# Second expert layer on Trainium2: the 64-token block contracted in two halves, side by side in the array

## The chip, the cores and the metric

One core of one Trainium2 chip runs the kernel. The metric is device microseconds of one launch: 1049.75 us, the median of three runs (1048.55 to 1050.27). Everything is float32 apart from small bfloat16 tiles of the assignment.

## The reference

The reference is an attention without softmax, followed by a mixture of experts in which each expert takes the same number of tokens. Only the last lines bear on the change: for each of E = 8 experts, the cap = 576 tokens that it was given go through two layers.

```python
out = np.einsum('bhsd,bhde->bhse', q, kv)          # kv = einsum('bhsd,bhse->bhde', k, v)
...
cap = N // E                                       # N 4608, E 8: cap 576
...
for e in range(E):
    mask = assigned == e
    h = np.maximum(x[mask] @ w1[e], 0.0)           # 576 x 512 by 512 x 1024
    out[mask] = h @ w2[e]                          # 576 x 1024 by 1024 x 512
```

## The kernel before

The kernel works in three stages. The **attention** (first 175 us) makes the tokens' rows and gate logits, batch by batch. Its last four token tiles are made of the last 64 tokens of two batches each: `token_tile` (L158) multiplies the two halves of such a tile, 64 tokens each, by the matrices `bd` of their two batches, and one half's result goes to partitions 0 to 63 of the PSUM tile `o_ps`, the other's to 64 to 127. The two halves alternate in the innermost loop. For the 32 other tiles one matmul has all 128 tokens. The **assignment** (to about 480 us) finds each token's expert, mostly on VectorE.

The **experts** follow, one after the other, and this is the stage that the change touches. An expert's 576 tokens are gathered in blocks of 128, 128, 128, 128 and 64 (list `blocks`), and turned by TensorE transposes (`turn`, L493) into `xt`. The first layer (L509) makes `hid`, 8 chunks of 128 units by 576 tokens, in matmuls of 288 columns. Then the next expert's tokens are turned and the tokens of the one after it gathered (`gather`, L482). The second layer (loop at L516) goes block by block: 8 matmuls, one for each chunk `f` of 128 of the 1024 units, add up in a PSUM tile `y_ps` of 512 columns (L519). The stationary operand is `hid` of the block's tokens, 128 or 64 columns wide, and the moving one is a chunk of `w2`. `take` moves the result to `y_sb`, and an indirect DMA writes it to the tokens' rows of the output (L523).

Two things set the order around the change. TensorE's instructions stand in the order in which the tile scheduler left them: an expert's second layer follows its first, with the next expert's transposes between the first blocks. And `take` gives every copy out of PSUM to ScalarE and VectorE in turn, by a counter that runs over the whole stage, so the number of copies in an expert decides which engine starts the next one. An expert has 16 copies of `hid`, 5 of `xt` and 5 of `y_sb`. The weights of expert e + 2 are loaded by SyncE as soon as the buffers of expert e are free (`load_w`, L189 and L191; two buffers each).

Each float32 matmul shows in the trace as two records on TensorE, each with a weight load of its own; the text calls such a record a pass.

Of the kernel before, what the change touches and what calls it, by code (L numbers as in the profile page):

```python
# [7 lines left out]
FT = mybir.dt.float32  # L8
# [3 lines left out]
AL = mybir.AluOpType  # L12
# [1 line left out]
AXX = mybir.AxisListType.X  # L14

P = 128
# Candidate thresholds that one counting step tries, and steps to a threshold: 17 ** -8 of the
# logits' range is below their last bit.
NCAND = 16
NSTEP = 8  # L20
NONE = -1.0e30
# [3 lines left out]
def kernel(  # L25
# [11 lines left out]
    nc = tc.nc  # L37
# [3 lines left out]
    N, DM = out.shape  # L41
    E, _, F = moe_w1.shape
    CAP = N // E
    NP = H // 2          # head pairs: two heads fill the 128 partitions
    J = 4                # consecutive tokens of a partition, in a batch's first 512
    G = J * P            # those tokens; the other S - G of two batches share a tile
    TL = S - G
    KP = 96              # k and v: S = 96 partitions of 6 rows
    KR = S // KP
    GC = N // P          # token tiles  # L50
    DC = DM // P
    FC = F // P
    W = 2 * (D + E)      # columns of a head pair: both kv, and both parts of the gate
    NB = (CAP + P - 1) // P
    HALF = CAP // 2
    assert TL * 2 == P and GC == B * J + B // 2 and HALF <= 512

    const = ctx.enter_context(tc.tile_pool(name="const", bufs=1, side="left"))
    wpool = ctx.enter_context(tc.tile_pool(name="wpool", bufs=2, side="left"))
# [5 lines left out]
    psa_cm = tc.tile_pool(name="ps_att", bufs=1, space=PS)  # L65
    psa = psa_cm.__enter__()

# [1 line left out]
    loaded = {}  # L69

    def load_kv(b):
# [25 lines left out]
    load_kv(1)  # L97
    load_q(1)

# [1 line left out]
    iota_p_i = const.tile([P, 1], I32, name="iota_p_i")  # L101
    nc.gpsimd.iota(iota_p_i, pattern=[[0, 1]], base=0, channel_multiplier=1)
    iota_p = const.tile([P, 1], FT, name="iota_p")
# [7 lines left out]
    nc.vector.tensor_scalar(gw.rearrange("p r l e -> p (r l e)"), in0=gw.rearrange("p r l e -> p (r l e)"),  # L111
                            scalar1=g_col, scalar2=None, op0=AL.mult)

    # Per batch and head pair, [kv, kv diag(g) w_gate], each with both heads on its diagonal.
    bd = att.tile([P, B, NP, W], FT, name="bd", bufs=1)
    nc.gpsimd.memset(bd[:, 0], 0.0)
    nc.gpsimd.memset(bd[:, 1:B], 0.0)
# [1 line left out]
    q_tail = att.tile([P, B // 2, H, D], FT, name="q_tail", bufs=1)  # L119
    lg = const.tile([P, E, GC], FT, name="lg")  # L120

# [1 line left out]
    def kv_product(b):  # L123
        k_sb, v_sb = loaded.pop(("k", b)), loaded.pop(("v", b))
        kv_ps = psa.tile([P, NP, D], FT, name="kv_ps", tag="kv")
# [15 lines left out]
        nc.vector.tensor_copy(bd[:, b, :, P:W], w_ps.rearrange("p r l e -> p r (l e)"))  # L141

    def token_tile(c, rows, batches, x_row):
        """rows(r): the tile's q of head pair r; batches: its one, or its two halves'."""
        qt_ps = psa.tile([P, NP, P], FT, name="qt_ps", tag="qt", bufs=2)
        for r in range(NP):
            nc.tensor.transpose(qt_ps[:, r, :], rows(r), ident)  # L147
        qt = att.tile([P, NP, P], FT, name="qt", tag="qt", bufs=3)
        if c % 2 == 0:
            nc.scalar.copy(qt, qt_ps)  # L150
        else:
            nc.vector.tensor_copy(qt, qt_ps)
        o_ps = psa.tile([P, NP, 256], FT, name="o_ps", tag="o", bufs=2)
        step = P // len(batches)
        for r in range(NP):
            for n, b in enumerate(batches):
                ps_ = slice(n * step, (n + 1) * step)
                nc.tensor.matmul(o_ps[ps_, r, 0:W], lhsT=qt[:, r, ps_], rhs=bd[:, b, r],  # L158
                                 start=True, stop=True)
        o_v = o_ps[:, :, 0:P]  # L160
        sq = att.tile([P, NP, P], FT, name="sq", tag="sq")
        nc.scalar.activation(sq, o_v, ACT.Square)  # L162
        ms = att.tile([P, H], FT, name="ms", tag="ms", bufs=3)
        nc.vector.reduce_sum(out=ms, in_=sq.rearrange("p r (l d) -> p (r l) d", l=2), axis=AXX)  # L164
        nc.vector.tensor_scalar(ms, in0=ms, scalar1=1.0 / D, scalar2=1.0e-6, op0=AL.mult, op1=AL.add)
        rt = att.tile([P, H], FT, name="rt", tag="rt", bufs=3)
        nc.scalar.activation(rt, ms, ACT.Sqrt)
        inv = att.tile([P, H], FT, name="inv", tag="inv", bufs=3)
        nc.vector.reciprocal(inv, rt)
        # One Newton step, as the table of the root is not exact.  # L170
        nc.vector.tensor_tensor(rt, inv, inv, op=AL.mult)
        nc.vector.tensor_tensor(rt, rt, ms, op=AL.mult)
        nc.vector.tensor_scalar(rt, in0=rt, scalar1=-0.5, scalar2=1.5, op0=AL.mult, op1=AL.add)  # L173
        nc.vector.tensor_tensor(inv, inv, rt, op=AL.mult)
        inv_h = inv.rearrange("p (r l o) -> p r l o", l=2, o=1)
        nc.vector.tensor_tensor(x_row.rearrange("p (r l d) -> p r l d", r=NP, l=2),
                                o_v.rearrange("p r (l d) -> p r l d", l=2),
                                inv_h.to_broadcast([P, NP, 2, D]), op=AL.mult)
        part = att.tile([P, NP, 2, E], FT, name="part", tag="part")
        nc.vector.tensor_tensor(part, o_ps[:, :, P:W].rearrange("p r (l e) -> p r l e", l=2),  # L180
                                inv_h.to_broadcast([P, NP, 2, E]), op=AL.mult)
        nc.vector.reduce_sum(out=lg[:, :, c], in_=part.rearrange("p r l e -> p e (r l)"), axis=AXX)

# [1 line left out]
    weights = {}  # L185

    def load_w(e):
# [34 lines left out]
    psa_cm.__exit__(None, None, None)  # L222
    att_cm.__exit__(None, None, None)

# [1 line left out]
    # Taking the logits from the highest down, until some expert is full: up to there every token  # L226
    # goes to its best expert that still has room. So E - 1 thresholds, in turn, and the rest.
    asg_cm = tc.tile_pool(name="asg", bufs=1, side="right")
    asg = asg_cm.__enter__()
    psr_cm = tc.tile_pool(name="ps_asg", bufs=1, space=PS)  # L230
# [17 lines left out]
    nc.vector.memset(inner, 1.0)  # L248
    nc.vector.memset(inner[:, :, 0:1], 0.0)

    # The logits' range, the same in every partition.
    ends = asg.tile([P, 2], FT, name="ends")
    lgf = lg.rearrange("p e c -> p (e c)")
    nc.vector.tensor_reduce(ends[:, 0:1], lgf, axis=AXX, op=AL.max)
# [35 lines left out]
        return asg.tile([P, w], dt, name=nm, tag="s_" + nm, bufs=2)  # L290

    def choose():
        """best: each token's best expert with room, of equals the first; mx: that logit, or
        below NONE / 2 for tokens that have their expert."""
        nc.vector.tensor_tensor(wl, lg, bc_e(shut), op=AL.add)
        nc.vector.tensor_reduce(mx, wl.rearrange("p e c -> p c e"), axis=AXX, op=AL.max)
        nc.vector.tensor_tensor(pick, wl, bc_c(mx), op=AL.is_ge)
        nc.vector.tensor_tensor(pick, pick, bc_e(code), op=AL.mult)
        nc.vector.tensor_reduce(code_mx, pick.rearrange("p e c -> p c e"), axis=AXX, op=AL.max)
        nc.vector.tensor_tensor(best, pick, bc_c(code_mx), op=AL.is_equal)  # L300
        nc.vector.tensor_tensor(mx, mx, gone, op=AL.add)

    def threshold():
        """[lo, hi) with an expert full when all at or above lo are taken, and none at hi."""
        lo, hi = bottom, top
        for _ in range(NSTEP):
            step = small("step")
# [26 lines left out]
        return lo, hi  # L334

    def ranks(own, sums):
        """For each token in `own`: one more than those before it of its partition, and how many
        there are in the partitions before."""
        here = asg.tile([P, E, GC], FT, name="here", tag="here", bufs=2)
        nc.vector.tensor_tensor_scan(here.rearrange("p e c -> p (e c)"), inner.rearrange("p e c -> p (e c)"),  # L340
                                     own.rearrange("p e c -> p (e c)"), 0.0, op0=AL.mult, op1=AL.add)
        ahead_ps = psr.tile([P, E], FT, name="ahead_ps", tag="end", bufs=2)
        nc.tensor.matmul(ahead_ps, lhsT=before, rhs=sums, start=True, stop=True)
        return here, ahead_ps

    def assign(lo, hi):
        """All at or above hi, and of those in [lo, hi) as many as their expert has room for."""
        two = asg.tile([P, 2, E, GC], BF, name="two", tag="two")
        cut = small("cut", GC)
        nc.vector.tensor_scalar(cut, in0=mx, scalar1=hi, scalar2=None, op0=AL.is_ge)  # L350
# [36 lines left out]
    nc.vector.tensor_tensor(pick, best, bc_c(rest), op=AL.mult)  # L387
    nc.vector.tensor_tensor(given, given, pick, op=AL.add)

# [1 line left out]
    sums_f = small("sums_f", 2 * E)[:, 0:E]  # L391
    nc.vector.reduce_sum(out=sums_f, in_=given, axis=AXX)
    sums = small("sums", 2 * E, BF)[:, 0:E]
# [17 lines left out]
    block = small("block", GC)  # L411
    nc.vector.tensor_copy(block, block_i)

    # The tokens' rows, in two numbers that bfloat16 holds.
    row_id = asg.tile([P, GC], I32, name="row_id")
    nc.gpsimd.iota(row_id[:, 0:B * J], pattern=[[S, B], [1, J]], base=0, channel_multiplier=J)
    nc.gpsimd.iota(row_id[:, B * J:GC], pattern=[[2 * S, B // 2]], base=G, channel_multiplier=1)
# [32 lines left out]
    psr_cm.__exit__(None, None, None)  # L450
    asg_cm.__exit__(None, None, None)

# [1 line left out]
    moe = ctx.enter_context(tc.tile_pool(name="moe", bufs=2, side="right"))  # L454
    psm = ctx.enter_context(tc.tile_pool(name="ps_moe", bufs=2, space=PS))

# [1 line left out]
    taken = {"n": 0}  # L458

    def take(dst, src, relu=False, scale=None):  # L460
        """Out of PSUM, on ScalarE and VectorE in turn."""
        taken["n"] += 1
        if taken["n"] % 2:
            if relu:
# [35 lines left out]
    for e in range(E):  # L500
# [14 lines left out]
            gather(e + 2)  # L515
        for n, (a, nr) in enumerate(blocks):  # L516
            y_ps = psm.tile([P, DM], FT, name="y_ps", tag="y")
            for f in range(FC):
                nc.tensor.matmul(y_ps[0:nr, :], lhsT=hid[:, f, a:a + nr], rhs=w2[:, f, :],  # L519
                                 start=(f == 0), stop=(f == FC - 1))  # L520
            y_sb = moe.tile([P, DM], FT, name="y_sb", tag="y", bufs=4)
            take(y_sb[0:nr, :], y_ps[0:nr, :])
            put = nc.gpsimd.indirect_dma_start(  # L523
                out=out, out_offset=bass.IndirectOffsetOnAxis(ap=ids[0:nr, e * NB + n:e * NB + n + 1], axis=0),
                in_=y_sb[0:nr, :], in_offset=None)
            tc.declare_no_dep(put.ins, group="rows_out", reason="every output row is written once")
            tc.add_to_no_dep_group("rows_out", put.ins)
# [30 lines left out]
```

## Time and profile before

| | |
|---|---|
| median of 3 runs | 1049.75 us (1048.55 to 1050.27) |
| span of the profiled execution, first to last instruction | 1045.8 us |
| its own time beside the span | the page gives none; the runs lie 2.8 to 4.5 us above the span |
| TensorE busy | 756.9 us (72%) |
| of it second layer, blocks of 128 tokens | 224.1 us in 512 passes |
| of it second layer, blocks of 64 tokens | 56.6 us in 128 passes |
| VectorE, ScalarE, GpSimd busy | 363.2, 98.7, 105.1 us |

The profile is one execution on the chip, and its span is the time between the first and the last instruction. Busy time of TensorE counts overlapping passes once. A group of rows names the source line, the engine, the operation, and output and input tiles.

### The profile page before, as it was taken

Reading aid. Unit: us, or ns where it says so; the run is one execution under the profiler, and the core shown is the slowest. Engines: PE = TensorE matmul, PEld = TensorE weight load, DVE = VectorE, ACT = ScalarE, POOL = GpSimd, SP = SyncE. Lnnn points to the kernel's source line nnn. Section 1 sums busy time; section 2 is a strip of 40 time slices with the busy share of each in tenths; the row PEclk is TensorE's granted clock in tenths of the full one; section 3 lists DMA queues with packets and bytes.
Section 4 is the critical chain, followed back from the end, with each engine's and each line's share of the span. In section 5 each row is a group of like instructions: output and inputs, shape, how many; then the busy total and the mean of one; then the engine's idle time right before and its main releaser. Section 6 shows DMA issues by size and latency. Waiting matters only on the chain.

```text
span 1045.8 us, 12692 instructions
## 1 busy us (share of the span) xinstructions
PE 756.9 (72%) x5277; PEld 509.7 (49%) x5277; DVE 363.2 (35%) x1295; ACT 98.7 (9%) x212; POOL 105.1 (10%) x132
## 2 busy tenths in 40 slices
PE   3796884223223223216999999999999999999996
PEld 3786874122212222213755747557466475574752
DVE  0666576565675666674110101101011011010100
ACT  1332231000000000000110101101001011010100
POOL 2211110000000000004120110210202100101001
PEclk9998796555555555555999999999999999999999
DMA  9999991000000000003133212330323122301000
GB/s 225 261 259 295 268 385 60 22 1 1 1 1 2 1 1 1 2 1 89 47 146 106 105 62 86 138 112 25 133 96 136 44 72 101 105 1 41 6 20 25
DMA packets 45721, 91.01 MB, mean 87 GB/s; under 512 B 7008, under 2 KB 27488, under 8 KB 44640
## 3 DMA queue, kind: packets, MB, share of 16 engines
q1 hardware_dynamic: 37632, 61.87, 20.8%
q0 software_dynamic: 7328, 28.32, 7.5%
q8 instruction: 41, 0.67, 0.3%
q10 hardware_dynamic: 704, 0.02, 0.1%
q14 instruction: 16, 0.13, 0.0%
HBM read 71.32 MB, written 18.87 MB: 86 GB/s over the span
## 4 chain that ended last, share of the span: by engine, by line
issue 50%; DVE 22%; PE 18%; POOL 6%; DMA 2%; ACT 2%; POOLq 0%; SPq 0%; DVEq 0%; ACTq 0%
PE n_ps L318 6%; PE o_ps L158 4%; DVE over L313 4%; POOL out_dram L523 4%; PE kv_ps L129 3%; POOL xg L482 2%; DVE cand L311 2%; DMA v_sb<-in_v_dram 1%; DVE up L328 1%; DVE step L308 1%; DVE hi L330 1%; PE qt_ps L147 1%; DVE lo L332 1%; PE k_ps L326 1%; DVE full L321 1%
## 5 line engine op out<-in xcount | busy, mean ns | idle before, releaser
L519 PE MATMUL y_ps<-w_sb,hid 128*128 128x512 f32 (+1 forms) x640 | 280.2, 594 | 0.0
L509 PE MATMUL h_ps<-xt,w_sb 128*128 128x288 f32 x1024 | 251.7, 408 | 0.0
L509 PEld LDWEIGHTS h_ps<-xt,w_sb 128*128 128x128 f32 x1024 | 194.5, 191 | 58.8 <-issue 5.7
L519 PEld LDWEIGHTS y_ps<-w_sb,hid 128*128 128x128 f32 (+1 forms) x640 | 112.5, 179 | 151.3 <-issue 150.7
L318 PE MATMUL n_ps<-best,over 128*16 128x8 bf16 x2016 | 62.5, 176 | 146.1 <-DVE over L313 105.5
L318 PEld LDWEIGHTS <-over 128*16 128x16 bf16 x2016 | 57.0, 89 | 173.9 <-DVE over L313 172.2
L471 DVE TENSOR_SCALAR hid<-h_ps 128x288 f32<-128x288 f32 x64 | 29.3, 458 | 253.2 <-PE h_ps L509 253.2
L475 DVE COPY y_sb<-y_ps 128x512 f32<-128x512 f32 (+1 forms) x17 | 11.8, 691 | 208.7 <-PE y_ps L519 208.7
L482 POOL DMA_INDIRECT xg<-x_dram,ids x40 | 37.9, 946 | 450.1 <-DVE ids L448 295.7
L158 PE MATMUL o_ps<-bd,qt 128*128 128x144 f32 (+1 forms) x320 | 54.9, 361 | 25.3 <-DVE rt L173 19.7
L523 POOL DMA_INDIRECT out_dram<-y_sb,ids x40 | 38.5, 964 | 323.6 <-ACT y_sb L469 189.4
L158 PEld LDWEIGHTS o_ps<-bd,qt 128*128 128x128 f32 (+1 forms) x320 | 49.2, 232 | 28.1 <-issue 24.7
L129 PE MATMUL kv_ps<-v_sb,k_sb 96*64 96x64 f32 x768 | 44.2, 242 | 14.4 <-DMA v_sb<-in_v_dram 14.4
L129 PEld LDWEIGHTS kv_ps<-v_sb,k_sb 96*64 96x64 f32 x768 | 41.4, 152 | 17.9 <-issue 16.2
L465 ACT ACTIVATE hid<-h_ps 128x288 f32<-128x288 f32 x64 | 26.3, 411 | 221.9 <-PE h_ps L509 221.9
L313 DVE TENSOR_TENSOR over<-mx,cand 128x576 bf16<-128x576 f32 x56 | 42.3, 755 | 1.5
L467 ACT ACTIVATE xt<-t_ps,g_col 128x512 f32<-128x512 f32 (+1 forms) x17 | 11.5, 675 | 326.3 <-DMA xg<-x_dram,ids 311.5
L469 ACT COPY y_sb<-y_ps 128x512 f32<-128x512 f32 (+1 forms) x23 | 13.4, 584 | 253.6 <-PE y_ps L519 253.6
L321 DVE SCALAR_TENSOR_TENSOR full<-n_ps,goal 16x8 f32<-16x8 f32 x56 | 8.6, 153 | 67.3 <-PE n_ps L318 67.3
L164 DVE TENSOR_REDUCE ms<-sq 128x8 f32<-128x512 f32 x36 | 24.6, 685 | 19.8 <-ACT sq L162 19.3
L162 ACT ACTIVATE sq<-o_ps 128x512 f32<-128x512 f32 x36 | 21.5, 597 | 73.1 <-PE o_ps L158 73.1
L473 DVE TENSOR_SCALAR xt<-t_ps,g_col 128x512 f32<-128x512 f32 (+1 forms) x23 | 15.4, 669 | 35.8 <-PE t_ps L493 33.8
(143 smaller groups left out, 471.6 us busy)
## 6 DMA issues: line engine op xcount, KB each, us to landing
w_sb<-in_moe_w_dram SPq DMA_DIRECT2D x16, 2048.0 KB, 9.7
k_sb<-in_k_dram SPq DMA_DIRECT2D x8, 1152.0 KB, 13.2
v_sb<-in_v_dram SPq DMA_DIRECT2D x8, 1152.0 KB, 18.1
q_sb<-in_q_dram SPq DMA_DIRECT2D x8, 1024.0 KB, 18.7
x_dram<-x_sb POOLq DMA_DIRECT2D x8, 1024.0 KB, 8.9
q_tail<-in_q_dram SPq DMA_DIRECT2D x8, 128.0 KB, 6.3
x_dram<-x_sb POOLq DMA_DIRECT2D x2, 512.0 KB, 5.4
xg<-x_dram,ids POOLq DMA_INDIRECT x40, 6.2
```

What stands on the lines that cost most here:

```text
L129: nc.tensor.matmul(kv_ps[ls, h // 2, :], lhsT=k_sb[:, h, j, :], rhs=v_sb[:, h, j, :], start=(j == 0), stop=(j == KR - 1))
L158: nc.tensor.matmul(o_ps[ps_, r, 0:W], lhsT=qt[:, r, ps_], rhs=bd[:, b, r], start=True, stop=True)
L162: nc.scalar.activation(sq, o_v, ACT.Square)
L164: nc.vector.reduce_sum(out=ms, in_=sq.rearrange("p r (l d) -> p (r l) d", l=2), axis=AXX)
L313: nc.vector.tensor_tensor(over, mx.rearrange("p (c o) -> p c o", o=1).to_broadcast([P, GC, NCAND]), cand.rearrange("p (o n) -> p o n", o=1 ...
L318: nc.tensor.matmul(n_ps, lhsT=over[:, c, :], rhs=best[:, :, c], start=(c == 0), stop=(c == GC - 1))
L465: nc.scalar.activation(dst, src, ACT.Relu)
L471: nc.vector.tensor_scalar(dst, in0=src, scalar1=0.0, scalar2=None, op0=AL.max)
L482: nc.gpsimd.indirect_dma_start(out=xg[0:nr, :], out_offset=None, in_=x_dram, in_offset=bass.IndirectOffsetOnAxis(ap=ids[0:nr, e * NB + n:e ...
L509: nc.tensor.matmul(h_ps, lhsT=w1[:, d, f * P:(f + 1) * P], rhs=xt[:, d, cs], start=(d == 0), stop=(d == DC - 1))
L519: nc.tensor.matmul(y_ps[0:nr, :], lhsT=hid[:, f, a:a + nr], rhs=w2[:, f, :], start=(f == 0), stop=(f == FC - 1))
L523: put = nc.gpsimd.indirect_dma_start(out=out, out_offset=bass.IndirectOffsetOnAxis(ap=ids[0:nr, e * NB + n:e * NB + n + 1], axis=0), in_=y ...
```

## The change

The 64-token block gets a branch of its own. Its 8 matmuls become 8 matmuls of the same shape, but the chunks of units 0 to 3 add up in partitions 0 to 63 of `y_ps`, and chunks 4 to 7 in partitions 64 to 127; the two alternate. Afterwards ScalarE copies the upper half to a new tile `y_part`, and VectorE adds it to the lower half into `y_sb`. The four 128-token blocks stay as they were. An expert thus has 25 copies that `take` counts, where it had 26. (The rest of the diff takes comments out and puts an assertion in.)

```diff
             y_ps = psm.tile([P, DM], FT, name="y_ps", tag="y")
-            for f in range(FC):
-                nc.tensor.matmul(y_ps[0:nr, :], lhsT=hid[:, f, a:a + nr], rhs=w2[:, f, :],
-                                 start=(f == 0), stop=(f == FC - 1))
             y_sb = moe.tile([P, DM], FT, name="y_sb", tag="y", bufs=4)
-            take(y_sb[0:nr, :], y_ps[0:nr, :])
+            if nr == P:
+                for f in range(FC):
+                    nc.tensor.matmul(y_ps, lhsT=hid[:, f, a:a + nr], rhs=w2[:, f, :],
+                                     start=(f == 0), stop=(f == FC - 1))
+                take(y_sb, y_ps)
+            else:
+
+                for f in range(FC // 2):
+                    for l in range(2):
+                        nc.tensor.matmul(y_ps[l * nr:(l + 1) * nr], lhsT=hid[:, l * FC // 2 + f, a:a + nr],
+                                         rhs=w2[:, l * FC // 2 + f, :], start=(f == 0), stop=(f == FC // 2 - 1))
+                y_part = moe.tile([P // 2, DM], FT, name="y_part", tag="y_part")
+                nc.scalar.copy(y_part, y_ps[nr:2 * nr])
+                nc.vector.tensor_tensor(y_sb[0:nr], y_ps[0:nr], y_part, op=AL.add)
```

On ScalarE, at the end of the first expert and through the second, the difference of the two programs' orders reads as follows (`h_ps`, `t_ps` and `y_ps` are the PSUM tiles of the first layer, the transposes and the second layer).

```order
 L467 ACTIVATE xt<-t_ps,g_col 128x4x128 x2
 L469 COPY y_sb<-y_ps 128x512 x2
-L469 COPY y_sb<-y_ps 64x512
+L531 COPY y_part<-y_ps 64x512
+L465 ACTIVATE hid<-h_ps 128x288 x8
+L467 ACTIVATE xt<-t_ps,g_col 128x4x128 x2
+L467 ACTIVATE xt<-t_ps,g_col 128x4x64
+L469 COPY y_sb<-y_ps 128x512 x2
+L531 COPY y_part<-y_ps 64x512
```

ScalarE keeps one instruction for the 64-token block, and every second expert it now has the copy of the short `xt` that VectorE had before.

On VectorE, at the end of the last expert, the addition stands in the place of a copy, and it comes after ScalarE's copy.

```order
 L471 TENSOR_SCALAR hid<-h_ps 128x288 x8
 L475 COPY y_sb<-y_ps 128x512 x2
-L475 COPY y_sb<-y_ps 64x512
-L553 UNCONDITIONAL_BRANCH
+L532 TENSOR_TENSOR y_sb<-y_ps,y_part 64x512
+L563 UNCONDITIONAL_BRANCH
```

The number of instructions before it is the same; the last one has a second input.

## Rows read from the trace of the kernel before

**Rows 1.** The page: engine totals, then the span in 40 slices.
```profile
PE 756.9 (72%) x5277; PEld 509.7 (49%) x5277; DVE 363.2 (35%) x1295; ACT 98.7 (9%) x212; POOL 105.1 (10%) x132
...
PE   3796884223223223216999999999999999999996
...
PEclk9998796555555555555999999999999999999999
```

**Rows 2.** Windows, nearly the whole experts' stage: length, busy time of each engine, clock.
```profile
526.00:1035.00 509.00, 509.00 (x1667) 295.85 (x1666) 49.88 (x93) 45.78 (x93) 60.81 (x64) 1.00 0.22 80
```

**Rows 3.** Groups by line and form, experts' stage: busy us, mean ns, idle before.
```profile
L519 PE MATMUL y_ps<-w_sb,hid 128*128 128x512 f32 x512 | 224.1, 594 | 0.0
...
L519 PE MATMUL y_ps<-w_sb,hid 128*64 128x512 f32 x128 | 56.6, 595 | 0.0
...
L519 PEld LDWEIGHTS y_ps<-w_sb,hid 128*64 128x64 f32 x128 | 16.9, 137 | 38.8 <-issue 38.8
```

**Rows 4.** Timeline of one 64-token block, expert 0: start us, us, instruction.
```profile
554.54 7.08 PE L519 MATMUL y_ps<-w_sb,hid 128*64 128x512 f32 x16
...
561.55 4.63 PE L509 MATMUL h_ps<-xt,w_sb 128*128 128x288 f32 x18
```

**Rows 5.** Timeline of the last block: weight loads, first and last of 14 single ones.
```profile
1029.05 0.14 PEld L519 LDWEIGHTS y_ps<-w_sb,hid 128*64 128x64 f32 x1 [0.29 <-issue]
...
1034.63 0.14 PEld L519 LDWEIGHTS y_ps<-w_sb,hid 128*64 128x64 f32 x1 [0.29 <-issue]
```

**Rows 6.** Windows of L158, a tile of one batch: PE busy (passes seen), PEld, clock.
```profile
28.40:28.60 0.20, 0.20 (x2) 0.20 (x2) 0.50 1.11 353
26.50:28.72 2.22, 1.98 (x9) 1.98 (x10) 0.61 1.08 316
26.50:28.96 2.46, 2.22 (x10) 2.22 (x11) 0.60 1.08 319
26.50:29.20 2.70, 2.46 (x11) 2.46 (x12) 0.59 1.08 323
...
141.40:141.72 0.32, 0.26 (x2) 0.29 (x3) 1.00 0.73 301
141.40:141.84 0.44, 0.38 (x3) 0.41 (x4) 1.00 0.80 317
141.40:141.96 0.56, 0.50 (x4) 0.54 (x5) 1.00 0.83 329
```

**Rows 7.** Windows of L158, tiles of two half batches; the same columns.
```profile
163.90:164.10 0.20, 0.14 (x2) 0.17 (x4) 0.50 0.00 0
163.90:164.34 0.44, 0.38 (x4) 0.41 (x6) 0.50 0.00 0
163.90:164.58 0.68, 0.62 (x6) 0.66 (x8) 0.50 0.00 0
...
170.90:173.90 3.00, 2.94 (x26) 2.97 (x28) 0.52 0.00 0
170.90:174.02 3.12, 3.06 (x28) 3.09 (x30) 0.54 0.00 0
170.90:174.14 3.24, 3.18 (x30) 3.21 (x32) 0.56 0.00 0
...
173.90:174.10 0.20, 0.20 (x8) 0.20 (x6) 1.00 0.00 0
```

**Rows 8.** Timeline, the end of the program.
```profile
1035.69 0.68 DVE L475 COPY y_sb<-y_ps 64x512 f32<-64x512 f32 x1 [13.19 <-PE y_ps L519]
1036.65 0.90 POOL L523 DMA_INDIRECT out_dram<-y_sb,ids  x1 [6.10 <-DVE y_sb L475]
```

**Rows 9.** Groups by line and form: prices of the copy and the addition.
```profile
L469 ACT COPY y_sb<-y_ps 64x512 f32<-64x512 f32 x7 | 4.1, 579 | 93.6 <-PE y_ps L519 93.6
...
L176 DVE TENSOR_TENSOR x_sb<-o_ps,inv 128x512 f32<-128x512 f32 x36 | 24.8, 688 | 1.4
```

**Rows 10.** Timeline of the attention's end: VectorE waits for ScalarE.
```profile
160.67 0.60 ACT L162 ACTIVATE sq<-o_ps 128x512 f32<-128x512 f32 x1 [1.00 <-PE o_ps L158]
...
161.30 0.69 DVE L164 TENSOR_REDUCE ms<-sq 128x8 f32<-128x512 f32 x1 [0.63 <-ACT sq L162]
```

**Rows 11.** DMA issues by line: KB each, median us to landing.
```profile
w_sb<-in_moe_w_dram SPq DMA_DIRECT2D x16, 2048.0 KB, 9.7
...
xg<-x_dram,ids POOLq DMA_INDIRECT x40, 6.2
out_dram<-y_sb,ids POOLq DMA_INDIRECT x40, 2.7
```

More of the change, by code (lines that the diff above doesn't have):

```diff
@@ L55 @@
     HALF = CAP // 2
-    assert TL * 2 == P and GC == B * J + B // 2 and HALF <= 512
+    assert CAP % P in (0, P // 2) and TL * 2 == P and GC == B * J + B // 2 and HALF <= 512
     const = ctx.enter_context(tc.tile_pool(name="const", bufs=1, side="left"))
```

## The prediction

> **What bounds the kernel now.** I first read the page's totals and its 40 slices. The totals call TensorE busy 72% of the span, an average over three stages. The slices split it: in the second half every slice of PE is a 9, at a granted clock of 9 or more, while the middle, the assignment, has PE at 2 or 3 [rows 1]. The change lies in the second half, so I asked for that stretch alone. In the 509 us from 526 to 1035 us TensorE is busy for 509.00 us, at clock 1.00, that is at 2.4 GHz; the four other engines have 46 to 61 us each, and the weight loads 296 us [rows 2]. Nothing else ends a wait there: TensorE is the bound, and a microsecond taken out of its queue is a microsecond off the end, until something else is late.
>
> Next the groups by form, since the mean over all forms would hide the point. Second-layer passes with 128 stationary columns and with 64 take the same 594 and 595 ns as records [rows 3]. A block of 64 tokens thus costs what one of 128 costs. The records overlap, so their lengths are not the pace. The pace is read from the weight loads, one to a pass: the first and last of 14 single ones begin at 1029.05 and 1034.63 us, so 5.58 / 13 = **0.429 us** a pass [rows 5]. Whole block: its first pass begins at 554.54, the next expert's first matmul at 561.55 us [rows 4], so 7.01 us, which is 16 x 0.429 = 6.86 and 0.15 for going into the narrow form and out of it.
>
> **The change, part by part.** *The matmuls.* Their number (16 passes a block, 8 blocks), shape and moving columns stay. Nothing is removed; the only possible gain is that two passes on different column halves run at once. The trace of before shows whether they do, in another place: the last four token tiles of the attention send 64 tokens to the lower half and 64 to the upper half of the same PSUM tile, alternating, in the same float32. I read it by windows that begin before the first pass and end at different times, so that the count tells how many passes have begun.
>
> First the control, a tile with all 128 columns. At clock 0.50 (1.2 GHz) the count goes 9, 10, 11 with every 0.24 us; at clock 1.00 it goes 2, 3, 4 with every 0.12 us [rows 6]. One pass at a time: 144 moving columns, 0.24 or 0.12 us. Then the half tiles: at clock 0.50 the count is 2, 4, 6 at 164.10, 164.34, 164.58, two with every 0.24 us, and two have begun already within the first window; the second pair of tiles, where the clock has risen to 1.00, goes 26, 28, 30 with every 0.12 us [rows 7]. Two passes begin where one did, at both levels of the clock, and the first two begin together. So the halves run fully beside each other here, with no offset that the view shows.
>
> I take this factor of two for the new block: 8 pairs x 0.429 = 3.43 us instead of 6.86, and the 0.15 us for the form stays. Saved: 3.43 us a block, 8 x 3.43 = **27.4 us**. What differs from the witness is the length, 512 columns for 144, and that four passes of a half add up in place; consecutive passes add up in place now at the full pace [rows 5]. Bounds of this term: 0 (no overlap) to 27.4 (two halves cannot give more than two).
>
> *The weight loads.* A pair needs two loads of 137 ns [rows 3]; one after the other 0.27 us, under the pair's 0.43, so they stay covered if they may run beside a pass. They do: before, each load lies within the 0.429 us between passes that follow without a gap [rows 2, 5], and in the half tiles, with two loads to 0.12 us, the pairs keep their pace [rows 7]. The Trainium skill speaks against this: "TensorE: Matmul & The Clock Gate", Part 3, says that weight loads overlap running matmuls only when they go to another group of rows, and here both halves use all the rows. By that rule the two loads would stand between pairs (the second rival). The trace disagrees with it at both places just named.
>
> *Copy and addition.* ScalarE's copy of 64 x 512 takes 579 ns [rows 9], as it does for seven of the eight blocks now. The addition with an operand in PSUM has no row at 64 partitions; VectorE's tensor-tensor from PSUM at 512 columns takes 688 ns, against 682 for the copy that it replaces [rows 8, 9], so I take 0.69; below nothing it can't go, and it would need 2 us to matter even once. In the first seven experts both lie under the next expert's first layer: ScalarE has 46 and VectorE 50 us of work in 509 [rows 2]. Behind them on these engines stand the first copies of the next `hid`, which are due every 1.9 us and have three buffers; the only follower of the addition is its own output DMA. Should that cover go, it would cost 0.6 us an expert, 5 us in all. In the last expert nothing covers it: copy, handover, addition follow the last pass, where one VectorE copy did. The handover from ScalarE to VectorE is 161.30 - 161.27 = 0.03 us [rows 10]. Added: 0.58 + 0.03 + 0.01 = **0.6 us**, on the path to the end.
>
> *The turn of `take`.* ScalarE and VectorE swap their copies in every second expert. Their work is a tenth of the stage [rows 2]; nothing, unless a transpose waits longer for its PSUM buffer, which I bound at 0.1 us an expert.
>
> *What could be late next.* An expert gets 3.4 us shorter, of 68. A weight load is issued a whole expert ahead and lands in 9.7 us, a gather in 6.2, an output in 2.7 [rows 11]. None comes near. The attention and the assignment are untouched.
>
> **Sum**, against the profiled execution: 1045.8 - 27.4 + 0.6 = 1019.0 us of span. The median of the runs is 1049.75, so 3.95 us lie around that span, and I add the same: **1023.0 us**. A measurement of this kernel tells about 0.2%, 2 us, from no change.
>
> **Rivals.**
>
> 1. *The pairs overlap, but imperfectly.* If a float32 matmul's own two passes must follow each other before the other half's first may begin, a block is 9 steps and not 8: 9 x 0.429 = 3.86, saving 3.0 x 8 = 24.0, time 1026.4. Against: the first two passes of the half tiles begin together [rows 7]. Or 512 columns hinder each other where 144 did not. If each half ran at four fifths, a block would be 3.43 / 0.8 = 4.29 us, the saving 2.57 x 8 = 20.6, the time 1029.8. For it speaks only that the witness at full clock is short, some 0.4 us. The Trainium skill has a figure of that size ("TensorE: Matmul & The Clock Gate", Part 3): three column tiles of 32 columns measured 2.38 times, four fifths of three.
>
> 2. *Weight loads uncovered.* A pair would be 0.43 + 0.27 = 0.70 us, a block 5.6, the saving 1.25 x 8 = 10, the time 1040.4. Rows 5 and 7 are against it.
>
> 3. *No overlap.* The passes go one after the other as now, and only the 0.6 us at the end is left: 1050.4, not to be told from no change. So it would also be if the halves did not alternate in the built program; in its order they do. Against: rows 7.
>
> 4. *Slower: a drain at each change of half.* If passes to the other half waited until the array was empty, each of a block's 7 changes would cost the rest of a record, 0.595 - 0.429 = 0.166 us, and nothing would overlap: 7 x 0.166 x 8 = 9.3 and 0.6, time 1059.7. With full overlap a change would have to cost 3.43 / 7 = 0.49 us to turn the sign. For it: going from 128 columns to 64 and back costs 0.15 us now [rows 4]. Against: rows 7, where halves alternate with no gap. The Trainium skill, "TensorEngine Tiling (Array Packing)", Key Properties, says that a change of the tiling mode drains the engine, and a change of tile does not; the 0.15 us agrees with the first half of that.
>
> **How the numbers follow.** Forecast (full pairs): 0.84, because the trace has the same pattern, type and half tiles at both clocks. Rival 1: 0.07, of which 0.04 for the 9 steps. Rival 2: 0.02. Rival 3: 0.04. Rival 4: 0.03. Faster 0.84 + 0.07 + 0.02 = 0.93, same 0.04, slower 0.03. The runs scatter by 1.7 us, the end of the program by some tenths, the swapped copies by 0.8 us: 1020.5 on the low side. On the high side the range takes in the 9 steps with 1 us of scatter: 1027.5. It holds 0.88 of the chance, less what scatter leaves out.
>
> **What would show it.** In windows over a narrow block the count of passes must rise by two with every 0.43 us, and the first pass of the block and the next expert's first matmul must lie 3.6 us apart instead of 7.01. An expert's period, first layer to first layer, must fall by 3.4 us. TensorE must stay busy throughout at clock 1.00. At the end a copy of 0.58 us and an addition of 0.69 must stand between the last pass and the last output. It would be wrong if the pairs stood further apart than 0.43 us, if single passes 0.43 us apart came back, or if an idle stretch opened before the next expert's first matmul.

## The result and the profile after

The changed kernel took **1020.12 us**, the median of 4 runs (1018.82 to 1022.23), against 1050.01 us for 4 runs of the kernel before: ratio 0.9736, 95% interval 0.9702 to 0.9769. It is faster. The median lies 0.4 us under the low end of the forecast range (1020.5 to 1027.5 us); the ratio lies inside it, as the range is 0.972 to 0.979 of the 1049.75 us from which it was worked out. The quotient of the two medians alone is 0.9715; the interval holds it too. Two of the 55 executions of the kernel before, at 1500 us with a granted clock of 0.55, are left out of every figure here.

Of the changed kernel's page, the totals and the slices that answer to [rows 1]; then two lines of its groups by form:

```profile
PE 727.5 (71%) x5277; PEld 498.6 (49%) x5277; DVE 366.6 (36%) x1299; ACT 100.7 (10%) x216; POOL 105.2 (10%) x132
...
PE   3797884223223223222899999999999999999995
...
PEclk9998796555555555555899999999999999999998
...
L528 PE MATMUL y_ps<-w_sb,hid 128*64 128x512 f32 x128 | 29.2, 598 | 0.0
...
L528 PEld LDWEIGHTS y_ps<-w_sb,hid 128*64 128x64 f32 x128 | 8.5, 136 | 19.8 <-issue 19.8
```

The number of TensorE instructions is the same, 5277, and its busy time is 29.4 us less. The MATMUL line shows where: the narrow blocks' 128 passes keep the length of a single record, 598 ns, but together they occupy 29.2 us instead of 56.6 [rows 3]. Each now lies on top of another one. The last line shows the same of their weight loads: 128 loads of 136 ns, 17.4 us one after the other, occupy 8.5 us, where they occupied 16.9 [rows 3].

One narrow block, by windows of its line that begin before the first pass (PE busy, passes seen, PEld, clock), as in [rows 7]:

```profile
554.00:554.30 0.30, 0.27 (x2) 0.20 (x4) 1.00 0.00 0
554.00:554.70 0.70, 0.67 (x4) 0.34 (x6) 1.00 0.00 0
554.00:555.10 1.10, 1.07 (x6) 0.49 (x8) 1.00 0.00 0
554.00:557.60 3.60, 3.57 (x16) 1.06 (x16) 1.00 0.19 73
```

The count goes up by two with every 0.43 us, and the first two are there together. The weight loads come in pairs as well, inside the 0.43 us: in the timeline of the last block each line has two of them, and the two together are 0.14 us long, so they lie beside each other; the engine that loads is idle for 0.29 us of each step.

```profile
1004.56 0.14 PEld L528 LDWEIGHTS y_ps<-w_sb,hid 128*64 128x64 f32 x2 [0.29 <-issue]
1004.99 0.14 PEld L528 LDWEIGHTS y_ps<-w_sb,hid 128*64 128x64 f32 x2 [0.29 <-issue]
```

How the span's 27.3 us (1045.8 to 1018.5) come together is read from the starts of first-layer matmuls in TensorE's timeline. Of the kernel before, the first of all, and the last expert's:

```profile
491.67 1.17 PE L509 MATMUL h_ps<-xt,w_sb 128*128 128x288 f32 x2
...
969.87 31.31 PE L509 MATMUL h_ps<-xt,w_sb 128*128 128x288 f32 x128
```

Of the changed kernel, the first of all, the first narrow block, then the first layers of experts 1, 2 and 7:

```profile
489.98 1.20 PE L509 MATMUL h_ps<-xt,w_sb 128*128 128x288 f32 x2
...
554.03 3.65 PE L528 MATMUL y_ps<-w_sb,hid 128*64 128x512 f32 x16
557.61 31.31 PE L509 MATMUL h_ps<-xt,w_sb 128*128 128x288 f32 x128
...
622.24 31.31 PE L509 MATMUL h_ps<-xt,w_sb 128*128 128x288 f32 x128
...
945.37 31.31 PE L509 MATMUL h_ps<-xt,w_sb 128*128 128x288 f32 x128
```

| stretch | before | after | difference |
|---|---|---|---|
| start to the first matmul of a first layer | 491.67 | 489.98 | -1.69 |
| expert 0 (to 561.55, 557.61) | 69.88 | 67.63 | -2.25 |
| experts 1 to 6 (to 969.87, 945.37) | 408.32 | 387.76 | -20.56 |
| expert 7 and the end | 75.93 | 73.13 | -2.80 |

Six experts give 20.56 / 6 = 3.43 us each, the forecast term to the hundredth. The last gives 0.63 less, the copy ahead of the addition:

```profile
1007.83 0.58 ACT L531 COPY y_part<-y_ps 64x512 f32<-64x512 f32 x1 [9.93 <-PE y_ps L528]
1008.45 0.68 DVE L532 TENSOR_TENSOR y_sb<-y_ps,y_part 64x512 f32<-64x512 f32 x1 [3.57 <-ACT y_part L531]
1009.40 0.90 POOL L533 DMA_INDIRECT out_dram<-y_sb,ids  x1 [3.28 <-DVE y_sb L532]
```

Expert 0 gives 1.2 us less, and the first stretch, which the change does not touch, differs by 1.7 us. Both are taken up below. Elsewhere nothing new waits: from 526 to 1007 us TensorE is busy throughout at clock 1.00.

```profile
526.00:1007.00 481.00, 481.00 (x1665) 287.17 (x1665) 53.16 (x96) 46.76 (x95) 60.37 (x63) 1.00 0.23 84
```

### The profile page after: what moved, and what is told of

Same layout as the page of the kernel before. It is cut to its first block, busy times and chain, and to the rows that moved or that the text cites. A ratio compares the mean times of both kernels' runs of the same rounds, so it can differ in the third digit from the quotient of the medians.

```text
span 1018.5 us, 12682 instructions
## 1 busy us (share of the span) xinstructions
PE 727.5 (71%) x5277; PEld 498.6 (49%) x5277; DVE 366.6 (36%) x1299; ACT 100.7 (10%) x216; POOL 105.2 (10%) x132
## 4 chain that ended last, share of the span: by engine, by line
issue 49%; DVE 23%; PE 17%; POOL 7%; DMA 2%; ACT 2%; POOLq 0%; SPq 0%; DVEq 0%; ACTq 0%
PE n_ps L318 6%; PE o_ps L158 5%; DVE over L313 4%; POOL out_dram L533 4%; POOL xg L482 3%; PE kv_ps L129 3%; DVE cand L311 2%; DMA v_sb<-in_v_dram 1%; DVE up L328 1%; DVE step L308 1%; PE qt_ps L147 1%; DVE hi L330 1%; DVE lo L332 1%; DVE full L321 1%; PE k_ps L326 1%
## 5 line engine op out<-in xcount | busy, mean ns | idle before, releaser
L521 PE MATMUL y_ps<-w_sb,hid 128*128 128x512 f32 x512 | 224.1, 594 | 0.0
L521 PEld LDWEIGHTS y_ps<-w_sb,hid 128*128 128x128 f32 x512 | 95.6, 190 | 112.5 <-issue 111.9
L471 DVE TENSOR_SCALAR hid<-h_ps 128x288 f32<-128x288 f32 x64 | 29.2, 457 | 209.6 <-PE h_ps L509 209.6
L475 DVE COPY y_sb<-y_ps 128x512 f32<-128x512 f32 x16 | 11.1, 692 | 182.1 <-PE y_ps L521 182.1
L158 PE MATMUL o_ps<-bd,qt 128*128 128x144 f32 (+1 forms) x320 | 53.7, 359 | 25.2 <-DVE rt L173 19.9
L158 PEld LDWEIGHTS o_ps<-bd,qt 128*128 128x128 f32 (+1 forms) x320 | 47.5, 226 | 28.4 <-issue 24.8
L528 PE MATMUL y_ps<-w_sb,hid 128*64 128x512 f32 x128 | 29.2, 598 | 0.0
L493 PEld LDWEIGHTS t_ps<-ident,xg 128*128 128x128 f32 (+1 forms) x160 | 18.5, 148 | 17.9 <-issue 8.2
```

The costliest lines, as they stand in the source:

```text
L471: nc.vector.tensor_scalar(dst, in0=src, scalar1=0.0, scalar2=None, op0=AL.max)
L521: nc.tensor.matmul(y_ps, lhsT=hid[:, f, a:a + nr], rhs=w2[:, f, :], start=(f == 0), stop=(f == FC - 1))
L528: nc.tensor.matmul(y_ps[l * nr:(l + 1) * nr], lhsT=hid[:, l * FC // 2 + f, a:a + nr], rhs=w2[:, l * FC // 2 + f, :], start=(f == 0), stop= ...
```

## The experiments

My theory: two passes on different column halves run at once and cost what one did, and nothing else in the change matters but 0.6 us at the end. Rivals that the result left open: that something else got faster too, since the first medians differ by 29.9 us and not 26.8; that the swapped copies matter; and that the order of the halves is not what gives the overlap.

### The changed kernel and the kernel before, once more

No edit. These runs and those of the later sections were made in three sessions, each on another chip.

> The changed kernel once more, with more rounds. My sum (27.4 us of passes saved, 0.6 us of copy and addition added) says 26.8 us less than the kernel before, ratio 0.9745. A rival that something else got faster too (the first medians differ by 29.9 us) says 29 to 30 us less, ratio 0.972 or below.

> The kernel before, unchanged, timed against itself: what the measurement calls no change. Expected ratio 1.000, within 0.2%. If executions of one kernel differ by 2 to 3 us, the 3 us by which the change did better than my sum are scatter. In its profile, time minus span tells whether 3.95 us lie around the span, as I assumed, or 1.8 as in the changed kernel's runs.

> The changed kernel a third time, beside the next run on the same chip: ratio to the kernel before between 0.972 and 0.975.

Measured: the changed kernel at ratio 0.9724 (0.9706 to 0.9741) and, in the other session, 0.9744 (0.9706 to 0.9781). The first interval ends just below my 0.9745 and holds the rival's 0.972, the second holds both. The kernel before against itself at 0.9999 (0.9982 to 1.0016), as expected, with single executions from 1041.85 to 1051.7 us over all sessions. All 15 runs of the changed kernel have a mean of 1019.6 us (standard error 0.7), 53 of the kernel before 1047.8 (0.3): a difference of 28.2 +- 0.7. My 26.8 is two standard errors away. So 1.7 of the 3.1 us of surplus in the first medians were scatter. In the first measurement and in the two sessions that have both kernels, the means differ by 29.7, 28.3 and 27.2 us.

Where the other 1.4 us lie, the profiles show: not in the stage that was changed. From the first matmul of a first layer to the end, the profiles of both kernels have:

| profile | first such matmul | end of span | between them |
|---|---|---|---|
| before, first profile | 491.67 | 1045.8 | 554.1 |
| before, taken here | 489.72 | 1044.9 | 555.2 |
| changed, first profile | 489.98 | 1018.5 | 528.5 |
| changed, second | 489.39 | 1017.4 | 528.0 |
| changed, third | 487.72 | 1014.9 | 527.2 |

The means differ by 26.8 us, the sum of the forecast. What stands ahead of that matmul the change does not touch, and it varies by itself: over all profiles in which it is the same program it is 482.9 (the run with the narrow block first) to 491.7 us long.

Time minus span is 1.8 us in these runs (1017.46 less 1015.7, 1046.66 less 1044.9). The profiled execution of the kernel before thus took some 1047.6 us, 2 us less than the median that I started from, and the 3.95 us around the span that I assumed were not there.

The profile of the kernel before taken here also explains expert 0. In the changed kernel's first expert, TensorE waits 1.7 us for VectorE to copy `hid`; the same late copy is in the kernel before, VectorE's timeline showing it at nearly the same place (the first line is the changed kernel's):

```profile
502.17 0.82 DVE L471 TENSOR_SCALAR hid<-h_ps 128x288 f32<-128x288 f32 x2 [8.06 <-PE h_ps L509]
```

```profile
501.78 0.89 DVE L471 TENSOR_SCALAR hid<-h_ps 128x288 f32<-128x288 f32 x2 [6.87 <-remote]
```

Two copies follow each other after 7 to 8 us of idleness, where every other comes 3.4 us after the last. The profile from which I predicted happened not to have it. Against the one taken here, whose expert 0 lasts from 489.72 to 560.64 us, the changed kernel's expert 0 is 3.29 us shorter. What holds VectorE there was not tried.

### The copies as they were shared before

```diff
                 nc.vector.tensor_tensor(y_sb[0:nr], y_ps[0:nr], y_part, op=AL.add)
+                taken["n"] += 1
```

> The changed kernel with the counter of copies advanced once more per narrow block, so that ScalarE and VectorE keep the copies that they had before the change. If the swapped copies cost nothing: the same as the changed kernel, within 0.2%, narrow block 3.6 us, expert's period 64.6 us. If the swap hides 1 us or more: that much slower or faster than the changed kernel.

Measured: 1020.91 us, ratio 0.9737 (0.9724 to 0.9749), which overlaps the changed kernel's in all sessions; the median is 1.7 us above the changed kernel's of the same session, within the 0.2% of the expectation. The narrow block, and the next expert's first layer, in TensorE's timeline:

```profile
554.70 3.65 PE L528 MATMUL y_ps<-w_sb,hid 128*64 128x512 f32 x16
558.28 31.31 PE L509 MATMUL h_ps<-xt,w_sb 128*128 128x288 f32 x128
...
622.91 31.31 PE L509 MATMUL h_ps<-xt,w_sb 128*128 128x288 f32 x128
```

The block takes 3.58 us and expert 1's period is 64.63 us, both as in the changed kernel (557.61 to 622.24). In this stage, who makes which copy costs nothing.

### The order of the halves

Three kernels change nothing but the order of the 8 narrow matmuls (lower half L, upper half U): first all of one half, then of the other; two and two; three and three. In the built programs the 8 matmuls of every narrow block stand in these orders.

```diff
-                for f in range(FC // 2):
-                    for l in range(2):
+                for l in range(2):
+                    for f in range(FC // 2):
```

> All four matmuls of the lower half, then all four of the upper half. If a matmul begins only after its predecessor has begun (order kept) and waits for its own half: the halves overlap at the seam alone, 14 steps of 0.429 us, narrow block 6.0 + 0.15 us, about 7 us less than the kernel before and 0.6 us back, ratio about 0.994. If the two passes of one matmul are queued apart: 15 steps, ratio 0.997. If TensorE reaches past waiting matmuls, it stays at 3.6 us a block and ratio 0.974.

Measured: 1033.23 us, ratio 0.9855 (0.9839 to 0.9871): none of the three. Half of the gain is left, and the windows show how (passes seen after PE busy):

```profile
552.80:554.40 1.60, 1.51 (x4) 0.60 (x5) 1.00 0.00 0
552.80:554.80 2.00, 1.91 (x6) 0.74 (x8) 1.00 0.00 0
552.80:555.30 2.50, 2.41 (x8) 0.99 (x10) 1.00 0.00 0
552.80:556.20 3.40, 3.31 (x12) 1.32 (x13) 1.00 0.20 77
552.80:558.10 5.30, 5.21 (x16) 1.73 (x16) 1.00 0.13 49
```

```profile
552.89 5.42 PE L528 MATMUL y_ps<-w_sb,hid 128*64 128x512 f32 x16
558.24 1.97 PE L509 MATMUL h_ps<-xt,w_sb 128*128 128x288 f32 x7
```

Four passes begin alone, then pairs, then four alone: 12 steps, 5.35 us. The upper half's first pass begins with the lower half's fifth, when three passes of the lower half that stand ahead of it have not begun. So TensorE doesn't keep strict order between the halves, and here it reached no further than three waiting passes. The Trainium skill, "TensorE: Matmul & The Clock Gate", Part 3, says that matmuls start strictly in the program's order; here they do not.

```diff
-                for f in range(FC // 2):
-                    for l in range(2):
+                for l, f in ((0, 0), (0, 1), (1, 0), (1, 1), (0, 2), (0, 3), (1, 2), (1, 3)):
+                    if True:
```

> The order lower, lower, upper, upper, twice. With order kept by whole matmuls (a matmul's two passes 2 steps, the next may begin right after it has begun if its half is free): 10 steps of 0.429 us, narrow block 4.3 + 0.15 us. With order kept by single passes: 13 steps, 5.6 + 0.15 us. With a reach past waiting matmuls: 8 steps, 3.6 us. In time against the kernel before: 20, 10 or 27 us less, ratios 0.981, 0.991, 0.975.

Measured: 1020.88 us, ratio 0.9730 (0.9705 to 0.9756), 8 steps; already the first window has two passes.

```profile
555.50:555.70 0.20, 0.16 (x2) 0.17 (x4) 1.00 0.00 0
```

That is what a reach of three makes: of L's four passes one runs and three wait, and U begins beside the first. The theory was made from the two runs, so a third tested it:

```diff
-                for f in range(FC // 2):
-                    for l in range(2):
+                for l, f in ((0, 0), (0, 1), (0, 2), (1, 0), (1, 1), (1, 2), (0, 3), (1, 3)):
+                    if True:
```

> The order lower x3, upper x3, lower, upper. Halves in a row took 12 steps, and the upper half began with the lower one's fifth pass, three passes of the lower half still waiting; two and two took 8. If three waiting passes of a half are what TensorE reaches past: the upper half begins with the third pass of the lower one, 10 steps of 0.429 us, narrow block 4.3 + 0.15 = 4.45 us, ratio to the kernel before 0.980. If it keeps the order of whole matmuls: 12 steps, 5.3 us, 0.986. If any order short of four in a row is as good as taking turns: 8 steps, 3.6 us, 0.973.

Measured: 1026.28 us, ratio 0.9812 (0.9774 to 0.9851). The windows, then the timeline of the block:

```profile
551.30:552.20 0.90, 0.81 (x2) 0.33 (x3) 1.00 0.00 0
551.30:552.60 1.30, 1.21 (x4) 0.52 (x6) 1.00 0.00 0
551.30:553.00 1.70, 1.61 (x6) 0.71 (x8) 1.00 0.00 0
```

```profile
551.39 4.56 PE L528 MATMUL y_ps<-w_sb,hid 128*64 128x512 f32 x16
555.88 10.45 PE L509 MATMUL h_ps<-xt,w_sb 128*128 128x288 f32 x42
```

Two passes begin alone, pairs follow, and the block takes 4.49 us against 4.45 expected: 10 steps, as the reach of three says. Whether TensorE looks three passes ahead in one queue, or keeps a short queue for each half, the three orders don't tell apart: both give 12, 8 and 10 steps.

| order | steps of 0.43 us | narrow block, us | ratio to before |
|---|---|---|---|
| one half alone (kernel before) | 16 | 7.01 | 1 |
| LLLL UUUU | 12 | 5.35 | 0.9855 |
| LLL UUU L U | 10 | 4.49 | 0.9812 |
| LL UU LL UU | 8 | 3.63 | 0.9730 |
| L U L U L U L U (the change) | 8 | 3.58 | 0.9736 |

### The narrow block first, in the last expert

```diff
-        for n, (a, nr) in enumerate(blocks):
+        order = list(enumerate(blocks))
+        for n, (a, nr) in (order[-1:] + order[:-1] if e == E - 1 else order):
```

> In the last expert alone the narrow block comes first, so that the last copy of the program is that of a 128-token block. If the copy and the addition at the end cost 0.6 us as in my sum: from the end of the last pass to the last output's issue 0.69 us of copy instead of 0.58 + 0.03 + 0.69, so 0.6 us less at that place; too little to tell in the times (ratio to the kernel before 0.974, as the changed kernel). If a 128-row output lands later than a 64-row one, it gives that back.

Measured: ratio 0.9734 (0.9709 to 0.9759), as the changed kernel. The end in its timeline:

```profile
1000.83 0.69 DVE L475 COPY y_sb<-y_ps 128x512 f32<-128x512 f32 x1 [13.04 <-PE y_ps L522]
1001.79 0.97 POOL L534 DMA_INDIRECT out_dram<-y_sb,ids  x1 [6.01 <-DVE y_sb L475]
```

From the first copy to the output's issue 0.96 us pass, in the changed kernel 1009.40 - 1007.83 = 1.57: the 0.6 us of the sum are there and can be had back. From that issue to the end of the span it is 9.2 us against 9.1, so 0.1 of it is returned; in the times it can't be seen.

### The attention's products by turns

In the attention, too, two heads' products lie in the two halves, but one after the other, with 12 passes of one half in a row.

```diff
-        for h in range(H):
-            ls = slice((h % 2) * D, (h % 2 + 1) * D)
-            for j in range(KR):
-                nc.tensor.matmul(kv_ps[ls, h // 2, :], lhsT=k_sb[:, h, j, :], rhs=v_sb[:, h, j, :],
-                                 start=(j == 0), stop=(j == KR - 1))
+        for r in range(NP):
+            for j in range(KR):
+                for l in range(2):
+                    nc.tensor.matmul(kv_ps[l * D:(l + 1) * D, r, :], lhsT=k_sb[:, 2 * r + l, j, :],
+                                     rhs=v_sb[:, 2 * r + l, j, :], start=(j == 0), stop=(j == KR - 1))
```

> The changed kernel, and in the attention the key-value products of two heads, which lie in the two column halves, take turns too instead of following each other. If halves overlap there as well: the passes of a head pair, 24 of 0.055 us, take half, so up to 48 x 2 x 0.055 / 2 = 2.6 us of TensorE less per batch, 21 us in all. But in the attention the DMA is busy at 0.96 of the span and TensorE at 0.73: if loads bound that stage, the time stays within 3 us of the changed kernel. A rival that TensorE's chain bounds the batch says 10 to 20 us less.

> The version in which the key-value products of two heads take turns as well, once more beside the changed kernel. If the 4 us by which it was ahead are real: ratio 0.968 to 0.971, and the attention's last logits 4 to 5 us earlier than in the changed kernel. If they were the scatter of the attention: the same ratio as the changed kernel, within 0.2%.

Measured: ratio 0.9690 (0.9668 to 0.9713) and 0.9696 (0.9655 to 0.9736). Over both sessions its 12 runs have a mean of 1015.4 us (standard error 0.9) against the changed kernel's 1019.6 (0.7): 4.2 +- 1.1 less. It is the fastest version. The attention's group of these matmuls in the changed kernel's first profile, and in the two of this version:

```profile
L129 PE MATMUL kv_ps<-v_sb,k_sb 96*64 96x64 f32 x768 | 43.9, 240 | 14.0 <-DMA v_sb<-in_v_dram 14.0
```

```profile
L129 PE MATMUL kv_ps<-v_sb,k_sb 96*64 96x64 f32 x768 | 31.3, 243 | 26.2 <-DMA v_sb<-in_v_dram 26.2
```

```profile
L129 PE MATMUL kv_ps<-v_sb,k_sb 96*64 96x64 f32 x768 | 33.4, 252 | 14.1 <-DMA v_sb<-in_v_dram 14.1
```

10 to 13 us of this group's TensorE time went, not the 21 that were expected at most, and 4 came off the time, between the expectation's two cases. Why these shorter passes (64 columns) do not gain the full factor of two was not tried; by the section on the order, halves in a row overlap at each change of half, so part of the gain may have been there before. In the first profile the gain turned into waiting for `v` (14 to 26 us); there the loads bound the stage, as half expected. The second does not show that wait, and the instruction that makes its last gate logits began at 175.0 us, the changed kernel's of that session at 174.9: the expected 4 to 5 us are not there. So how the 4 us come about is open. In the profiles with the attention unchanged that instruction began between 170.1 and 179.1 us, a scatter larger than the effect.

## Why the prediction was right

- *Bound.* TensorE without a gap in the stretch of [rows 2]; so it is still, and the block's saving went through to the end in all seven experts that have a successor. (Two slips that changed nothing: the last slice of [rows 1] is a 6, and [rows 2] has three other engines, not four.)
- *Pairs at full pace.* Taken from the half tiles [rows 7], 3.43 us a block forecast; 3.43 an expert measured over six. The length of 512 columns and the adding up in place changed nothing.
- *9 steps.* Fell: 8 steps, the first two passes together.
- *Uncovered weight loads.* Fell: two loads of 0.14 us in each step of 0.43, with no gap between the pairs. The prediction had the two one after the other, 0.27 us; they lie beside each other, 0.14 us for both, so there was more room than it thought.
- *Drain at each change of half.* Fell by the same rows. The form's 0.15 us stayed: 3.58 - 3.43.
- *Copy and addition.* 0.58 + 0.04 + 0.68 after the last pass; 0.6 us more than before forecast, 0.63 measured.
- *Swapped copies.* Nothing that shows in the stage, by the run that keeps them.
- *Time around the span.* Wrong: 1.8 us, not 3.95. The profiled execution was a short one. The forecast difference was laid on the median, so it did not suffer; the 1023.0 us did, as that median of three runs is 2 us above the mean of 53.
- *Range.* Too tight below. It allowed 1.7 us of scatter, from three runs; single executions of the kernel before spread over 9.85 us, and 10 of the 15 of the changed kernel lie below 1020.5 us. As a ratio to the kernel before, measured beside it, the range holds; the absolute time hung on the base as well, which says nothing for or against the mechanism.
- *Against the runs.* The forecast difference of 26.8 us is small against 28.2 +- 0.7; the parts of the profile that the change touches give 26.8 (7 x 3.43 + 2.80, with the late copy of expert 0 left out), and so does the whole stage over five profiles. What is over lies ahead of the stage, where executions differ by themselves.

## What to carry to other kernels

A matmul with 64 stationary columns cost here what one with 128 costs (595 and 594 ns); a second one on the other column half ran beside it for nothing, in float32, at both levels of the clock. Look for a place in the trace where the halves already take turns: it prices the change before it is made. Let the halves alternate in the program, at least two and two; by its steps, three in a row cost a quarter of the gain here, four in a row half of it. And ask whether TensorE bounds the stage: where it did, all of the gain came off the time; in the attention, under busy loads, the gain itself was half of what was hoped, and a third of it came off, by a way that stayed open.

## What was not expected of the hardware

TensorE let a matmul of the free half begin ahead of up to three waiting passes of the busy half. That came out of three orders of the same 8 matmuls (12, 10 and 8 steps), one of them forecast from the other two. That holds for this shape, two column halves and float32 matmuls of two passes each; others were not tried. Nor was it expected that the weight loads of the two halves lie beside each other: 128 of them, 136 ns each, occupy 8.5 us.
